# New orders for the first loads, stage A and the first full block of stage B in a two-attention kernel

## The chip, the cores and the metric

The kernel runs on one core of a Trainium2 chip. The metric is the device time of one execution in microseconds (us), as the median of several runs. The engines are TensorE (PE in the profile, with PEld for its weight loads), the vector engine (DVE), ScalarE (ACT), GpSimd (POOL) and SyncE (SP), which issues all transfers of this kernel.

## The reference

Two multi-head attentions on separate inputs, A and B, with 2048 tokens, width 512 and 32 heads of 16. A is causal with a sliding window of 256 tokens; B is full attention. The results stand side by side in the output.

```python
qkv = (x @ wqkv).reshape(B, S, 3, H, Dh).transpose(2, 0, 3, 1, 4)
q, k, v = qkv[0], qkv[1], qkv[2]
scores = einsum("bhqd,bhkd->bhqk", q, k) * Dh ** -0.5
# A only: key 0 to 255 tokens behind the query
scores = where((i - j >= 0) & (i - j < 256), scores, -1e9)
o = einsum("bhqk,bhkd->bhqd", softmax(scores), v)
y = o.transpose(0, 2, 1, 3).reshape(B, S, D) @ wo
out = concatenate([yA, yB], axis=-1)
```

All inputs are float32.

## The kernel before

**Tiling.** The tokens of each attention are cut into 4 chunks of 512 and 16 tiles of 128. Heads go in 8 groups of four. A *unit* is one attention, one group and one query chunk: 32 units of A, then 32 of B. Float32 accuracy comes from splitting each operand into a high part (a copy in a reduced format, on ScalarE) and a low part (the rest, a subtraction on DVE or GpSimd); a projection multiplies high by high, high by low and low by high over four blocks of 128 inputs, 12 matmuls in all (`products`, line 217 in the profile). The splits of A's first tiles are lines 170 (ScalarE) and 171 (DVE), and the loads that feed them line 185 (`load_split`).

**Steps.** A projection of queries or keys (`project_qk`) leaves its result in PSUM, ScalarE copies it out (line 275 for the first pair), the two parts are stored to DRAM, and loads bring them back laid out by head. Values (`project_v`) go through DRAM as well. For each unit, query times key matmuls are first done to find each row's maximum on DVE (line 454 for A, with lines 463 and 464; line 406 for B, with DVE's maximum in line 410), the negated maxima become extra rows of the query operand (a transpose, line 539 or 492), and then the scores are multiplied again with those rows (line 572), ScalarE takes the exponential (line 579), and the weighing with the values follows (line 603 for B, 618 for A). Output projections (`project_out`) run on TensorE between the scores of B; they use line 217 too.

**Stage A and its order.** `ORDER_A` is a string with one letter for each piece of TensorE's work: p a projection, m maxima of two heads, t the transposed rows of maxima, s the scores of two heads, w a weighing, e and S early work of B. `ORDER_P` names the projections in the order in which the p's take them: "Av20" is attention A, values, chunk 2, tile 0; "Ak01" is A, keys, pair 0, chunk 1. So TensorE's order is written out by hand. The order on ScalarE, DVE, GpSimd and SP is not: while the program is built, the class `Model` keeps an estimated time for each engine, and a step behind a load or a projection (a split, a copy out, a store, a load) is put into the program when the model's TensorE time has passed the step's own estimated time. Every engine then executes its instructions in that program order, waiting for whatever each needs. `Model.dma` estimates when a load lands: 0.45 us for its issue, 0.6 us more, 4 ns for each KB, and 1.3 us at the end.

**The first loads.** The list "load" is worked off in order: query weights of pair 0, the four 128-row tiles of token chunk 0 (as 1, 1 and 2), key weights of pair 0, constants, then two loads each of two tiles for chunk 1, two for the values' weights, and two for each of chunks 2 and 3. The tiles of two use staging buffers with the tag "p", of which there are six (`2 * AHEAD`), and a seventh load waits until the first of them has been split.

**Stage B and its order.** Here the order comes from short strings that are repeated. `ORDER` covers two key tiles (eight scores, two steps); "s" is the scores of one head, "M" the maxima of two heads in a fixed pair of banks (3 and 4), "m" the maximum of one head in a bank that it shares with the output projections, a digit a weighing of that many quarters, "T" the rows of maxima, and "x" one matmul of an output projection. `ORDER_F` covers eight steps with 12 x, and it is taken at each multiple of eight steps as long as an output projection is due. After 12 x one more matmul of the projection is issued. The first output projection is due from step 24 on. 16 blocks of `ORDER_F` follow one another from there, and then `ORDER` again. `ORDER_B`, `ORDER` without its last M, is for the block at two steps ahead of such a multiple, when a projection is due by then.

Of the kernel before, what the change touches and what calls it, by code (L numbers as in the profile page):

```python
# [20 lines left out]
HG = 4  # L21
# [17 lines left out]


ORDER = "ssm4mssMs2msms2TsM"
ORDER_B = "ssm4mssMs2msms2Ts"
ORDER_F = "msMs2mssm2ssMms4ssMms4ssMms4ssMsm4ssMms4mssMsxxxxxxTxxMsmss4MssmsxxxxsMsms4s"
LAST = "ssss4T"
LAST_F = "xxxxssss44ssssxxxxxxssss44ssssxx"
# [2 lines left out]


ORDER_P = (  # L50
# [4 lines left out]
    "Bk31 Bq30 Bq33 Bq32 Bq20 Bk23 Bk30 Bq31 Bk11 Bk33 Bk32 Bq12 ").split()  # L55
FIRST = 4.0
FINAL = 34.5
LOADS = 4.0
# [4 lines left out]


ORDER_A = (
    "pppppppmpmmpmmpmmmptpmmpmmpsmspmmpmsppmmpmmmpmmtpmsswmmmpsmswtmmpmswssmpmmtpmswmsmpmsswsmwssmpmswmss"
    "wtmmpsmmpsmwmmmpmsmwsmwsstpsmswmmmpsmswwssmpsmsptwsmmpmsmwwmsmpsmsptsmwmsmwsmsmsmwssmmwtssmwmmmpmswm"
    "msptsmmswmmmpmmswsmsmwsmtwsspssmwmmmpmsswtmswmsmpmsswmmswsmmptssmwmmspmsmwmswmsmpsmswmmmptmsmmmpmsmw"
    "smmswmswstmmpmsmsmwsmwsmssmwtmmmpmsmsmwssmwsmtswsmmpmswsmswmmtpsmswmmmpmsswmmmpmmtpsmswwmssptmswsmmw"
    "sspmswmmmpmsswsmtpmmswsmwsmmpmsssmwsmswmmtpssmwmmmpsmswmmmpsmswwsmmptsmwmsmpmsmwmsptsmwmsmpsmsptmswm"  # L70
    "mmpssmwmsmwsmsmwmsmptsmwmsmpsmswmmmpssmwmmmpssmtwwssmpmsswsmwsmmptsewmmmpsempsmswsemwsmptsewmmmpemsp"
    "mmswsmtwssepssmwmmmpempesswemmpssmwwsesptsmwemmpesmwmmpssmwsseptmsmpmmmpesmwsmwsmmpemmpmmmpemmpssmws"
    "mmptsmwmmmpSmSwmSmwSm")
LAND = 700
LATE = 1000
LAND_V = 2000
# [3 lines left out]


WAKES = {"PE": 226, "ACT": 243, "DVE": 219, "Pool": 200, "SP": 200, "DMA": 200}
TURN = {("f", "h"): 90, ("h", "f"): 85, ("h", "c"): 88, ("c", "h"): 115, ("c", "f"): 115, ("f", "c"): 105, ("c", "c"): 24}


class Model:
# [4 lines left out]
    def __init__(self):  # L91
        self.t = {e: 0 for e in ("PE", "ACT", "DVE", "Pool", "SP", "DMA")}
        self.mode, self.turn = "f", 170
        self.banks = {"e": [0] * 7, "o": [0]}
        self.lanes = [0] * 8

    def run(self, engine, ns, *after):
        self.t[engine] = max(self.t[engine], *after, 0) + ns
# [8 lines left out]
        self.mode = mode  # L107
        return self.run("PE", turn + ns, *after)

    def dma(self, kb, *after):  # L110
        t = self.run("SP", 450, *after, self.lanes[0]) + 600
        self.t["DMA"] = max(self.t["DMA"], t) + int(4.0 * kb)

        self.lanes = [*self.lanes[1:], self.t["DMA"] + 1300]
        return self.lanes[-1]
# [33 lines left out]
def attention_kernel(ctx: ExitStack, tc: tile.TileContext, xT, wqk, wv, wo, out):  # L149
# [9 lines left out]
    M = Model()  # L159
    ready = {}  # L160
    obank = [None]
    ns = 0
# [14 lines left out]
    def load_split(srcs, tags, d, keys, stage):  # L177

        slots = staged[stage]
        if stage == "p":  # L180
            r = sb.tile([128, 2, QC], F32, name=f"in_{keys[0]}".translate(NAMES), tag=stage, bufs=2 * AHEAD)
        else:
            r = sb.tile([128, QC], F32, name=f"in_{keys[0]}".translate(NAMES), tag=stage,
                        bufs=5 if stage == "row" else 3)[:, None]
        nc.sync.dma_start(r[:, :len(keys)], srcs)
        t = M.dma(256 * len(keys), slots.pop(0))

        def rest():
            for n, (tag, key) in enumerate(zip(tags, keys)):
                d[key] = sb.tile([128, 2, 512], F32R, name=f"{tag[0]}_{key}".translate(NAMES), tag=tag[0], bufs=tag[1])  # L190
                split(r[:, n], d[key], nc.gpsimd if stage == "stage" else nc.vector, key[:2] == (1, "o"))
                ready[tag[0], *key] = M.run(*(("Pool", 1260) if stage == "stage" else ("DVE", 602)),
                                            M.run("ACT", 500, t))
            slots.append(ready[tag[0], *key])
        after(t + (LAND_X if stage == "stage" else 0), rest, (stage, *keys[0]))
# [674 lines left out]
        list_("load", yes, free("p"), load_x, 0, 0, i, n)  # L870
    list_("load", yes, free("row"), load_wqk, 0, 0, 1)
    list_("load", yes, at0, constants)
    for n, f, *a in [(0, load_x, 0, 1, i, 2) for i in (0, 2)] + [(0, load_wv, 0, i, 2) for i in (0, 2)] + [
            (EARLY + 4 * (c - 2), load_x, 0, c, i, 2) for c in (2, 3) for i in (0, 2)]:
        list_("load", lambda n=n: nb >= n, free("p"), f, *a)
    list_("load", lambda: nb >= 12, at0, ones_out)
# [69 lines left out]
    nm = k = nb = ne = n1 = 0  # L946
# [18 lines left out]
    while todo_a or gen[0]:  # L965
# [8 lines left out]
        i, j = divmod(ns, HG)  # L974
        t = NEVER
        if gen[0]:
            t = pe
        elif x == "p":
            t = max(bank(), operands(bursts[nb][1]))
        elif x == "t" and nts:  # L980
            t = max(ready["nm", *nts[0]], bank())
        elif x == "w" and k < i:
            un, (m, pieces), a, z = flat[k]
            t = max(*(ready.get(("v", 0, un[1] // 2, y[0]), NEVER) for y in pieces), ready["p", *un, m],
                    M.bank("o") if a else 0)
        elif x == "s" and i < k + AHEAD and (max_rows, *flat[i][0]) in made:
            t = max(M.bank("e", 1), ready["q", *flat[i][0]] + LAND)
        elif x == "S" and ns == HG * len(flat) and len(flat) + n1 // HG < k + AHEAD and (max_rows, 1, 0, 0) in made:
            t = max(M.bank("e", 1), ready["q", 1, 0, 0] + LAND)
# [3 lines left out]
        elif x == "m" and not (mxs[nm][2] and (nts or mxs[nm][0][0] and ne < len(early))):  # L993
# [3 lines left out]
            t = max(t, M.pair()[0])  # L997
# [91 lines left out]
    ns, nq, nm, fed = n1, n1 - 8, AHEADM, 0  # L1089
    half, odd, full = 2 * AHEADM, None, set()  # L1090
    t0 = M.t["PE"] - 1000 * ns // HG * STEP
    rows, order = [], ORDER
    for u, g, c, qt, kc in mx[:AHEADM]:
        chunk_max(g, c, qt, kc)

    def due():
        return gen[0] or proj and proj[0][0] <= ns // HG * STEP and operands(proj[0][3]) <= M.t["PE"]

    while nq < 4 * len(steps):
        if nm == len(mx) and len(M.banks["e"]) == 3:  # L1100
            M.banks["e"] += [M.t["PE"] + 4000] * 2
        if nm == len(mx):
            order = LAST_F if due() and not rows else LAST
        else:
            f, g = order == ORDER_F, ns // HG % 8
            order = ORDER_F if due() and g == 0 and nm + 8 <= len(mx) else ORDER
            if order == ORDER and not f and g == 6 and due() and nm + 10 <= len(mx):
                order = ORDER_B
        for x in order:
            k = ns // HG  # L1110
            if x == "s" and k < len(steps):
                if ns % HG == 0:
                    t = k * STEP
                    M.t["PE"] = max(M.t["PE"], t0 + int(1000 * k * STEP))
                    settle()
                    while todo and todo[0][0] <= t:
                        pop()
                scores(1, *steps[k], ns % HG)
                ns += 1
            elif x in "Mm" and (half < 2 * len(mx) or x == "m" and odd is not None):  # L1120
                if x == "M":
                    y = half
                    half += 1
                    max2(*mx[y // 2][1:], (2 * (y % 2), 2 * (y % 2) + 1), ps_all[:, 3:5])
                elif odd is None:
                    y, odd = half, half
                    half += 1
                    max2(*mx[y // 2][1:], (2 * (y % 2),), room()[1][:, None])
                else:
                    y, odd = odd, None  # L1130
                    max2(*mx[y // 2][1:], (2 * (y % 2) + 1,), room()[1][:, None])
                if y != odd:
                    full.add(y)
                while {2 * nm, 2 * nm + 1} <= full:
                    u, g, c, qt, kc = mx[nm]
                    chunk_max(g, c, qt, kc)
                    nm += 1
                    if nm % 16 == 0:
                        low_finish(g, c)
                        rows.append((k + 1, (1, g, c)))  # L1140
            elif x == "T":
                if rows and rows[0][0] + (nm == len(mx)) <= k:
                    max_rows(*rows.pop(0)[1])
            elif x == "x" and (gen[0] or due()):
                now[0] = k * STEP
                advance()
                fed += 1
                if fed == 12:
                    fed = 0
                    advance()  # L1150
                    if nm < len(mx):
                        t0 += 2410
            elif x.isdigit():
                if 0 <= nq < 4 * len(steps):
                    g, c, kt = steps[nq // 4]
                    q = nq % 4
                    weigh2(g, c, kt, 128 * q, 128 * (q + int(x)))
                    if kt == NT - 1 and q + int(x) == 4:
                        unit_end(1, g, c)
                nq += int(x)  # L1160
# [29 lines left out]
```

## Time and profile before

| what | value |
|---|---|
| median of 3 runs | 1818.7 us (1818.28 to 1819.19) |
| the profiled execution, its own time | 1819.65 us |
| its span, first to last instruction | 1817.9 us |
| mean granted TensorE clock | 0.998 |
| first matmul | 10.19 us into the span |
| stage A | to about 535 us |
| stage B | from about 535 us on |
| maxima of B end | at about 1730 us |

Times in the profile count from the start of the span; the 1.75 us between the span and the execution's own time lie around it. A busy TensorE in the profile is not TensorE at its peak, since matmuls are pipelined and their ends are modelled. The granted clock is a share of the full clock.

### The profile page before, as it was taken

The numbers are of one execution on the slowest core, as the hardware profiler recorded it, in microseconds if no ns is written. First come the engines' busy times: TensorE is split into PE (matmuls) and PEld (weight loads), VectorE is DVE, ScalarE is ACT, GpSimd is POOL, SyncE is SP. The second block draws the span as 40 slices with busy tenths as digits, with TensorE's granted clock in tenths as the row PEclk, the third lists the DMA queues.
The fourth block names the chain that finished last, engine by engine and source line by source line (L and its number), as shares of the span: only waits on it lengthen the run. The fifth ranks groups of instructions, "written<-read, shape, count | busy, mean of one in ns | idle before, by whom it ended". The sixth has DMA issues, their size and how long they took to land. (4 is left out here: it accounts for less than half of the span.)

```text
span 1817.9 us, 38163 instructions
## 1 busy us (share of the span) xinstructions
PE 1798.2 (99%) x13992; PEld 901.4 (50%) x13992; DVE 1515.2 (83%) x2189; ACT 1420.0 (78%) x2773; POOL 688.8 (38%) x2054
## 2 busy tenths in 40 slices
PE   7999999999999999999999999999999999999999
PEld 5766666666664444444444444444444444444446
DVE  4655676766689889999989999999999999999911
ACT  4367777565659788888889988998898998899883
POOL 0167787554655453223222423332222333222310
PEclk9999999999999999999999999999999999999999
DMA  7756767454553225111300311030030121000012
GB/s 239 198 177 200 225 206 220 152 164 140 180 182 104 71 74 117 45 42 40 75 28 26 74 47 39 29 78 17 16 76 29 35 63 37 17 24 15 30 34 97
DMA packets 128569, 166.47 MB, mean 92 GB/s; under 512 B 22946, under 2 KB 58258, under 8 KB 128370
## 3 DMA queue, kind: packets, MB, share of 16 engines
q1 hardware_dynamic: 128382, 164.04, 31.2%
q8 instruction: 110, 1.80, 0.4%
q14 instruction: 77, 0.63, 0.1%
HBM read 94.49 MB, written 68.19 MB: 89 GB/s over the span
## 5 line engine op out<-in xcount | busy, mean ns | idle before, releaser
L579 ACT ACTIVATE p<-ps_all 128x512 f32<-128x512 f32 x2432 | 1257.8, 598 | 163.1 <-PE ps_all L572 116.0
L410 DVE TENSOR_REDUCE mt<-ps_all 128x1 f32<-128x512 f32 (+1 forms) x1482 | 1203.4, 884 | 53.3 <-PE ps_all L406 38.2
L572 PE MATMUL ps_all<-oq,opk 51*128 51x512 f32 (+3 forms) x2752 | 739.4, 406 | 2.4 <-ACT p L579 2.1
L406 PE MATMUL ps_all<-opk,oq 48*128 48x512 f32 x2016 | 636.3, 433 | 1.0 <-DVE mt L410 1.0
L603 PE MATMUL ps_all<-p,vt 128*32 128x256 f32 (+1 forms) x5672 | 586.8, 487 | 0.0
L572 PEld LDWEIGHTS ps_all<-oq,opk 51*128 51x128 f32 (+1 forms) x2752 | 376.8, 185 | 227.7 <-ACT p L579 196.0
L406 PEld LDWEIGHTS ps_all<-opk,oq 48*128 48x128 f32 x2016 | 303.1, 185 | 277.7 <-issue 149.7
L517 POOL TENSOR_TENSOR md<-mt,mm 128x4 f32<-128x4 f32 x372 | 75.9, 204 | 612.2 <-DVE mt L410 611.2
L589 POOL TENSOR_SCALAR_AFFINE_SELECT p<-p 128x256 f32<-128x256 f32 x480 | 178.9, 406 | 221.9 <-ACT p L579 220.4
L603 PEld LDWEIGHTS ps_all<-p,vt 128*32 128x32 f32 x5672 | 112.7, 108 | 218.1 <-issue 208.1
L217 PE MATMUL ps_all<-x,w 128*128 128x512 f32 x768 | 195.1, 404 | 10.3 <-ACT w L170 10.2
L463 DVE COPY_PREDICATED ps_all<-mone,ps_all 128x256 f32<-128x256 uint16 x224 | 95.0, 424 | 85.8 <-PE ps_all L454 84.1
L217 PEld LDWEIGHTS ps_all<-x,w 128*128 128x128 f32 x768 | 141.2, 190 | 50.5 <-ACT w L170 10.2
L464 DVE TENSOR_REDUCE mt<-ps_all 128x2 f32<-128x512 f32 x224 | 155.2, 693 | 7.7
L279 ACT ACTIVATE raw<-ps_all 128x512 f32<-128x512 f32 x56 | 33.5, 598 | 108.8 <-PE ps_all L217 105.9
L217 PE MATMUL ps_all<-w_o,x_o 128*128 128x512 f32 x384 | 102.3, 407 | 0.2 <-ACT ob L715 0.2
L217 PE MATMUL ps_all<-w_v,x 128*128 128x512 f32 x384 | 96.4, 400 | 0.3 <-DVE w_v L171 0.3
L618 PE MATMUL ps_all<-p,vt 128*32 128x384 f32 (+2 forms) x1408 | 96.4, 390 | 0.0
L518 POOL TENSOR_SCALAR md<-md 128x4 f32<-128x4 f32 x372 | 81.7, 220 | 32.6
L454 PE MATMUL ps_all<-opk,oq 48*128 48x384 f32 (+2 forms) x512 | 88.1, 373 | 1.3 <-DVE mt L464 1.1
L519 POOL TENSOR_TENSOR mm<-mm,md 128x4 f32<-128x4 f32 x372 | 74.8, 201 | 31.0
L217 PEld LDWEIGHTS ps_all<-w_o,x_o 128*128 128x128 f32 x384 | 68.0, 188 | 26.9 <-issue 8.0
(63 smaller groups left out, 718.3 us busy)
## 6 DMA issues: line engine op xcount, KB each, us to landing
parts<-st SPq DMA_DIRECT2D x64, 512.0 KB
opk<-parts SPq DMA_DIRECT2D x128, 128.0 KB
oq<-parts SPq DMA_DIRECT2D x128, 128.0 KB
od<-ou SPq DMA_DIRECT2D x64, 256.0 KB
vd<-vst SPq DMA_DIRECT2D x32, 272.0 KB
opk<-parts SPq DMA_DIRECT2D x128, 64.0 KB
oq<-parts SPq DMA_DIRECT2D x128, 64.0 KB
t<-od SPq DMA_DIRECT2D x32, 256.0 KB
```

What stands on the lines that cost most here:

```text
L217: nc.tensor.matmul(ps, l(u), r(v), start=start and k == 0, stop=stop and k == n - 1)
L406: nc.tensor.matmul(ps[:, n], q[rows, 128 * qt:128 * qt + 128], k[rows, kc * QC:kc * QC + QC], start=True, stop=True)
L410: nc.vector.tensor_reduce(out=m[:, a:a + len(heads), r, qt, kc], in_=ps, axis=AX.X, op=ALU.max)
L454: nc.tensor.matmul(two[:, a, 0:w], opq[b, g, c][rows, r, 128 * qt:128 * qt + 128], opk2(g)[rows, r, t0:t1], start=True, stop=True)
L463: nc.vector.copy_predicated(two[:, :, 256:384], later, two[:, :, 0:128])
L464: nc.vector.tensor_reduce(out=m[:, :, r, qt, 0], in_=two[:, :, 128:384], axis=AX.X, op=ALU.max)
L518: nc.gpsimd.tensor_scalar(d, d, 0.0, None, op0=ALU.max)
L572: nc.tensor.matmul(ps[x][:, col:col + n1], opk2(g)[rows, pr, 128 * k:128 * k + 128], opq[b, g, c][rows, pr, q0:q0 + n1], start=True, stop= ...
L579: nc.scalar.activation(p[:, a0 + x, :w], ps[x][:, :w], AF.Exp, scale=SCALE)
L589: nc.gpsimd.affine_select(out=v, in_=v, pattern=[[0, 2], [sign, 128]], compare_op=ALU.is_ge, fill=zero_fill, base=base, channel_multiplier ...
L603: nc.tensor.matmul(o[32 * j:32 * j + 32, q0:q1], vt[(g // 2) % 2][:, kt, vc:vc + 32], pts[1, g, c, kt, j // 2][:, j % 2, q0:q1], start=kt ...
L618: nc.tensor.matmul(o[32 * j:32 * j + 32, q0:q0 + w], vt[(g // 2) % 2][:, kt, vc:vc + 32], pts[b, g, c, m, j // 2][:, j % 2, col:col + w], ...
```

## The change

The values' weights are loaded ahead of token chunk 1 instead of behind it. `Model` gets a table of landing times for the first nine loads that go through `load_split`, in place of its formula. `ORDER_A` and `ORDER_P` are replaced. `ORDER_B` goes, and the first block that would be `ORDER_F` is `ORDER_F1` instead; the later ones stay.

```diff
--- before.py
+++ after.py
@@ -39,7 +39,7 @@
 
 
 ORDER = "ssm4mssMs2msms2TsM"
-ORDER_B = "ssm4mssMs2msms2Ts"
+ORDER_F1 = "ssm4msMss2msms2sMssm4ssmMs4mssm3mssMm14sssmMxxxxxxmssMsxTxxxxxsmMss2smms2sMssm4s"
 ORDER_F = "msMs2mssm2ssMms4ssMms4ssMms4ssMsm4ssMms4mssMsxxxxxxTxxMsmss4MssmsxxxxsMsms4s"
 LAST = "ssss4T"
 LAST_F = "xxxxssss44ssssxxxxxxssss44ssssxx"
@@ -48,11 +48,11 @@
 
 
 ORDER_P = (
-    "Ak00 Aq00 Av00 Av11 Aq01 Av20 Ak01 Aq02 Av02 Av33 Av13 Ak02 Av03 Av01 Ak03 Av31 Aq03 Av22 Av23 Av21 Av10 "
-    "Av12 Ak10 Av30 Ak11 Av32 Ak20 Ak13 Ak12 Aq10 Aq11 Aq12 Aq13 Aq20 Ak30 Ak21 Aq31 Aq30 Aq32 Aq21 Ak31 Ak23 "
-    "Bk00 Aq22 Ak32 Ak22 Aq33 Aq23 Ak33 Bq01 Bk01 Bq00 Bk02 Bk03 Bq02 Bv00 Bv33 Bv21 Bv31 Bv01 Bq13 Bk10 Bv32 "
-    "Bk13 Bq10 Bk12 Bq03 Bv02 Bv22 Bv13 Bv12 Bv30 Bq21 Bv23 Bk22 Bv20 Bv11 Bq11 Bv03 Bv10 Bk20 Bk21 Bq23 Bq22 "
-    "Bk31 Bq30 Bq33 Bq32 Bq20 Bk23 Bk30 Bq31 Bk11 Bk33 Bk32 Bq12 ").split()
+    "Aq00 Ak00 Av11 Av00 Ak01 Av01 Aq01 Ak02 Av03 Av21 Av33 Aq02 Av02 Aq03 Av12 Av10 Ak03 Av30 Av32 Av23 Av20 "
+    "Av13 Ak10 Ak11 Av22 Av31 Ak20 Aq12 Ak30 Ak12 Aq10 Ak13 Aq13 Aq11 Aq21 Aq30 Aq22 Aq20 Ak22 Aq31 Aq32 Ak21 "
+    "Ak31 Bk00 Ak32 Ak33 Ak23 Aq33 Aq23 Bk01 Bq01 Bq03 Bk02 Bk03 Bq00 Bv12 Bv22 Bv00 Bq02 Bv21 Bk21 Bv11 Bq13 "
+    "Bv31 Bv03 Bq12 Bk10 Bk20 Bv01 Bk13 Bq10 Bv10 Bv23 Bv20 Bv02 Bq23 Bk22 Bv13 Bv33 Bk23 Bq20 Bv32 Bv30 Bk11 "
+    "Bk12 Bq30 Bk30 Bk31 Bq31 Bq33 Bq11 Bk32 Bq21 Bk33 Bq32 Bq22 ").split()
 FIRST = 4.0
 FINAL = 34.5
 LOADS = 4.0
@@ -63,14 +63,14 @@
 
 
 ORDER_A = (
-    "pppppppmpmmpmmpmmmptpmmpmmpsmspmmpmsppmmpmmmpmmtpmsswmmmpsmswtmmpmswssmpmmtpmswmsmpmsswsmwssmpmswmss"
-    "wtmmpsmmpsmwmmmpmsmwsmwsstpsmswmmmpsmswwssmpsmsptwsmmpmsmwwmsmpsmsptsmwmsmwsmsmsmwssmmwtssmwmmmpmswm"
-    "msptsmmswmmmpmmswsmsmwsmtwsspssmwmmmpmsswtmswmsmpmsswmmswsmmptssmwmmspmsmwmswmsmpsmswmmmptmsmmmpmsmw"
-    "smmswmswstmmpmsmsmwsmwsmssmwtmmmpmsmsmwssmwsmtswsmmpmswsmswmmtpsmswmmmpmsswmmmpmmtpsmswwmssptmswsmmw"
-    "sspmswmmmpmsswsmtpmmswsmwsmmpmsssmwsmswmmtpssmwmmmpsmswmmmpsmswwsmmptsmwmsmpmsmwmsptsmwmsmpsmsptmswm"
-    "mmpssmwmsmwsmsmwmsmptsmwmsmpsmswmmmpssmwmmmpssmtwwssmpmsswsmwsmmptsewmmmpsempsmswsemwsmptsewmmmpemsp"
-    "mmswsmtwssepssmwmmmpempesswemmpssmwwsesptsmwemmpesmwmmpssmwsseptmsmpmmmpesmwsmwsmmpemmpmmmpemmpssmws"
-    "mmptsmwmmmpSmSwmSmwSm")
+    "pppppppmmppmmpmmmpmpmmptpmmpmmpssspmmpmmpsmtpmsswmmmpsmmpmmmptmswmsmpwmmsptmswmsmpsmswsmwmmmpmsspmms"
+    "wsmwmsmptmswssmpmsmwsmwssmptmswmmmpmsswmstwmsspwmmmpmsspmmswwmsmpsmsptsmmwsmmswsmswtsmmswmsswmmpsmsw"
+    "mmpmsstwmmmpmswsmmswsstwmspsmswmmmpsmmswmsmwmsptsmswmmmpmsmwtmsswsmmpsmsmwmmmptsmsmwmmmpssmwmmmptsmm"
+    "swssmwmsmwsmpmssmwsmstwmssmwmmmpmssmwmsmwtssmwmsmpmsmwsmptsmwmsmpssmwmmmpsmswsmmptmswmswsmmptmswmsmp"
+    "msswsmwmsmpmmswsmwmsmptssmwmsmpsmswsmswmmtpsmswmmmpsmswssmwwsmmptmswsmmpmswsmmpmmswsmptsmwmsmpmswmsm"
+    "pmswmmmpsssptmmptsmwsmswsmswmmmpssmwmmmpsmswwmsmptmswmmmpsmwmsmpseswmmspsseptsmwmmmpemmpsmswtmswmmmp"
+    "tsmwmmmpssepseswseswmmmpesswemmptsesmwwmmmpesspmmswsmwmmmpssmwmmmptseswemmpemmpemmpseswsempsmswmmmpm"
+    "mmptsmswsmmpSmSwSmwSm")
 LAND = 700
 LATE = 1000
 LAND_V = 2000
@@ -80,6 +80,7 @@
 
 
 WAKES = {"PE": 226, "ACT": 243, "DVE": 219, "Pool": 200, "SP": 200, "DMA": 200}
+LANDINGS = 3500, 5400, 6100, 8300, 9300, 10400, 11800, 13200, 14600
 TURN = {("f", "h"): 90, ("h", "f"): 85, ("h", "c"): 88, ("c", "h"): 115, ("c", "f"): 115, ("f", "c"): 105, ("c", "c"): 24}
 
 
@@ -93,6 +94,7 @@
         self.mode, self.turn = "f", 170
         self.banks = {"e": [0] * 7, "o": [0]}
         self.lanes = [0] * 8
+        self.landings = list(LANDINGS)
 
     def run(self, engine, ns, *after):
         self.t[engine] = max(self.t[engine], *after, 0) + ns
@@ -107,9 +109,11 @@
         self.mode = mode
         return self.run("PE", turn + ns, *after)
 
-    def dma(self, kb, *after):
+    def dma(self, kb, *after, first=False):
         t = self.run("SP", 450, *after, self.lanes[0]) + 600
         self.t["DMA"] = max(self.t["DMA"], t) + int(4.0 * kb)
+        if first and self.landings:
+            self.t["DMA"] = self.landings.pop(0) - 1300
 
         self.lanes = [*self.lanes[1:], self.t["DMA"] + 1300]
         return self.lanes[-1]
@@ -183,7 +187,7 @@
             r = sb.tile([128, QC], F32, name=f"in_{keys[0]}".translate(NAMES), tag=stage,
                         bufs=5 if stage == "row" else 3)[:, None]
         nc.sync.dma_start(r[:, :len(keys)], srcs)
-        t = M.dma(256 * len(keys), slots.pop(0))
+        t = M.dma(256 * len(keys), slots.pop(0), first=True)
 
         def rest():
             for n, (tag, key) in enumerate(zip(tags, keys)):
@@ -870,7 +874,7 @@
         list_("load", yes, free("p"), load_x, 0, 0, i, n)
     list_("load", yes, free("row"), load_wqk, 0, 0, 1)
     list_("load", yes, at0, constants)
-    for n, f, *a in [(0, load_x, 0, 1, i, 2) for i in (0, 2)] + [(0, load_wv, 0, i, 2) for i in (0, 2)] + [
+    for n, f, *a in [(0, load_wv, 0, i, 2) for i in (0, 2)] + [(0, load_x, 0, 1, i, 2) for i in (0, 2)] + [
             (EARLY + 4 * (c - 2), load_x, 0, c, i, 2) for c in (2, 3) for i in (0, 2)]:
         list_("load", lambda n=n: nb >= n, free("p"), f, *a)
     list_("load", lambda: nb >= 12, at0, ones_out)
@@ -1089,7 +1093,7 @@
     ns, nq, nm, fed = n1, n1 - 8, AHEADM, 0
     half, odd, full = 2 * AHEADM, None, set()
     t0 = M.t["PE"] - 1000 * ns // HG * STEP
-    rows, order = [], ORDER
+    rows, first = [], True
     for u, g, c, qt, kc in mx[:AHEADM]:
         chunk_max(g, c, qt, kc)
 
@@ -1102,10 +1106,10 @@
         if nm == len(mx):
             order = LAST_F if due() and not rows else LAST
         else:
-            f, g = order == ORDER_F, ns // HG % 8
+            g = ns // HG % 8
             order = ORDER_F if due() and g == 0 and nm + 8 <= len(mx) else ORDER
-            if order == ORDER and not f and g == 6 and due() and nm + 10 <= len(mx):
-                order = ORDER_B
+            if order is ORDER_F and first:
+                order, first = ORDER_F1, False
         for x in order:
             k = ns // HG
             if x == "s" and k < len(steps):
```

## The prediction

> **What bounds the kernel now.** I read the page first (span and busy engines), then the waits of TensorE, then busy time and granted clock by stretch, then the order of time at the two places where TensorE stands still longest.
>
> ```profile
> span 1817.9 us, 38163 instructions
> PE 1798.2 (99%) x13992; PEld 901.4 (50%) x13992; DVE 1515.2 (83%) x2189; ACT 1420.0 (78%) x2773; POOL 688.8 (38%) x2054
> ...
> PE ps_all L217 <- ACT w L170: 10.2, 1, 10.2
> PE ps_all L572 <- ACT p L579: 2.1, 8, 0.5
> PE ps_all L454 <- DVE mt L464: 1.1, 3, 0.5
> PE ps_all L406 <- DVE mt L410: 1.0, 1, 1.0
> ```
>
> TensorE is busy in 99% of the span, and only 19.7 us (1817.9 less 1798.2) are left. So a new order gains only what it takes out of TensorE's waits or out of its slow stretches. Two waits stand out: 10.2 us before the first matmul, put down to the split of a weight tile, and one of 1.0 us on the maxima of the vector engine (DVE). All other waits are 0.5 us at most.
>
> ```profile
> 45.00:535.00 490.00, 487.62 (x3720) 324.17 (x3718) 329.14 (x680) 299.98 (x591) 292.17 (x571) 1.00 0.61 185
> ...
> 182.00:273.00 91.00, 89.17 (x718) 57.46 (x717) 66.37 (x156) 65.30 (x131) 71.14 (x126) 1.00 0.72 215
> 364.00:455.00 91.00, 90.99 (x728) 60.54 (x730) 60.51 (x135) 53.70 (x104) 45.71 (x104) 1.00 0.49 152
> ...
> 592.00:595.90 3.90, 2.90 (x24) 1.34 (x20) 3.90 (x5) 2.24 (x4) 3.58 (x6) 1.00 0.61 146
> 595.90:602.73 6.83, 6.83 (x36) 2.25 (x36) 3.96 (x6) 3.88 (x8) 4.60 (x11) 0.50 0.10 35
> ```
>
> These are stretches: length, then busy time of PE, PEld, DVE, ACT and POOL, then clock. The first row is stage A, in which TensorE idles 2.4 us in 490; the worst 91 us of it idle 1.83 us, a good stretch 0.01. The last two rows are the only slow stretch: right behind the 1.0 us wait, the granted clock is 0.50 for 6.83 us, so half of that, 3.4 us, is lost there.
>
> **The change, part by part.**
>
> *The start.* The first projection was Ak00 and becomes Aq00. The row of waits names the weight tile of Ak00, which is loaded fifth; the weights of Aq00 are loaded first.
>
> ```profile
> 3.67 0.63 ACT L170 ACTIVATE w<-in 128x512 fp32r<-128x512 f32 x1 [1.61 <-DMA in<-wqk_A]
> 5.58 1.29 ACT L170 ACTIVATE x<-in 128x512 fp32r<-128x512 f32 x2 [1.28 <-DMA in<-xT_A]
> 8.47 1.15 ACT L170 ACTIVATE x<-in 128x512 fp32r<-128x512 f32 x2 [1.60 <-DMA in<-xT_A]
> 9.53 0.61 ACT L170 ACTIVATE w<-in 128x512 fp32r<-128x512 f32 x1
> 10.49 1.15 ACT L170 ACTIVATE x<-in 128x512 fp32r<-128x512 f32 x2 [0.35 <-DMA in<-xT_A]
> 11.85 1.15 ACT L170 ACTIVATE x<-in 128x512 fp32r<-128x512 f32 x2 [0.22 <-DMA in<-xT_A]
> 15.76 0.60 ACT L275 ACTIVATE st<-ps_all 128x512 fp32r<-128x512 f32 x1 [2.75 <-PE ps_all L217]
> 16.25 1.14 ACT L170 ACTIVATE w_v<-in_v 128x512 fp32r<-128x512 f32 x2
> ...
> 6.24 1.36 DVE L171 TENSOR_TENSOR x<-in,x 128x512 fp32r<-128x512 f32 x2 [1.22 <-ACT x L170]
> 9.13 1.29 DVE L171 TENSOR_TENSOR x<-in,x 128x512 fp32r<-128x512 f32 x2 [1.54 <-ACT x L170]
> 10.34 0.68 DVE L171 TENSOR_TENSOR w<-in,w 128x512 fp32r<-128x512 f32 x1
> ...
> 10.19 8.32 PE L217 MATMUL ps_all<-x,w 128*128 128x512 f32 x24 [10.19 <-ACT w L170]
> 18.35 1.87 PE L217 MATMUL ps_all<-w_v,x 128*128 128x512 f32 x7
> 24.49 2.88 PE L217 MATMUL ps_all<-x,w 128*128 128x512 f32 x12
> ...
> 10.19:15.52 5.33, 5.33 (x13) 4.01 (x14) 1.00 1.05 392
> 15.52:18.35 2.83, 2.83 (x14) 2.31 (x12) 1.00 0.29 111
> ```
>
> The first three parts are ScalarE, DVE and TensorE in order of time; the last two rows are line 217 by stretch. One projection is 12 matmuls. The first takes 5.33 us (0.444 us each), the second 2.83 (0.236 each): TensorE starts at about half pace, although the clock column has no drop. The same four projections stand first in both orders (Ak00, Aq00, Av00, Av11), and before they end at 24.49.
>
> Aq00 can start when the first token tile's high part is there, 6.24 instead of 10.19. At slow pace it ends at 6.24 + 5.33 = 11.6; the fourth tile's low part is there at 9.13 + 1.29 = 10.4, in time. Ak00's weights are there at 10.34 + 0.68 = 11.0, so it ends at 14.4 at the full pace and at 17.0 at the slow one. Next is Av11, which needs the second token chunk. Here the moved load counts: its 2 transfers go past the 2 of the chunk on SP's queue, and 4 splits on ScalarE and 4 on DVE change places with the chunk's 4 and 4. The chunk's halves were split on landing at 10.49 and 11.85, 1.36 apart; two transfers later they come at 13.2 and 14.6. The seventh load still waits for a free staging buffer, now the chunk's second half in place of the weights' second half: the same wait in the same place. ScalarE's splits of the last half take 1.15 us, DVE's end 0.7 later, so about 16.4, or 17.0 if ScalarE first takes Ak00's result (0.6). So Av11 ends about 17.5 (last tile at 17.0 plus two matmuls), Av00 2.8 later at 20.3: a gain of 4.2. With Ak00 at the slow pace to 17.0, ScalarE stands behind it as it did at 15.76 (2.75 us idle), the chunk is split by 19.6, Av11 ends at 20.1 and Av00 at 22.9: a gain of 1.6. I take **3.2**, a little nearer to the first, since the slow pace ended 5.3 us behind the first matmul, but the new first matmuls lie farther apart. What the weights gain by their earlier split (16.25 before) is in this sum. All later work follows these projections, and TensorE is full behind them, so I let the gain go through to the end.
>
> [...]
>
> *The landing table.* It changes no instruction, only where ScalarE, DVE and SP take their work in the program: nothing by itself, beyond the start and stage A as costed.
>
> *The order of stage A.* The counts are equal (96 projections, 284 maxima, 192 scores, 96 weighings, 33 rows), and changes of matmul kind go from 366 to 365. Projections are only permuted. If all of stage A idled as its good stretch does, it would gain 2.4 us; if all of it idled as its worst (1.83 in 91), it would idle 9.9 us, a loss of 7.5. With the same counts I take **0**. What hides the moved work is PSUM's seven banks; without them each maximum waits for DVE as below.
>
> *The first full block of stage B.* ORDER_F1 takes the place of ORDER_F once; ORDER_B goes. ORDER_B was for a block at step 22 with an output projection due, but the first is due at step 24, and the trace has the closing M which ORDER_B leaves out: zero.
>
> ```profile
> 591.46 0.64 PE L603 MATMUL ps_all<-p,vt 128*32 128x256 f32 x8
> 592.03 0.94 PE L406 MATMUL ps_all<-opk,oq 48*128 48x512 f32 x3
> 592.81 0.40 PE L572 MATMUL ps_all<-oq,opk 51*128 51x512 f32 x1
> 594.21 0.50 PE L406 MATMUL ps_all<-opk,oq 48*128 48x512 f32 x2 [1.00 <-DVE mt L410]
> ...
> 592.81:618.66 25.85, 10.73 (x32) 4.84 (x32) 0.87 0.12 36
> 618.66:639.65 20.99, 9.40 (x33) 4.41 (x32) 1.00 0.32 102
> 639.65:661.62 21.97, 9.43 (x33) 4.43 (x32) 1.00 0.33 79
> 1100.00:1118.80 18.80, 10.68 (x32) 5.32 (x32) 1.00 0.05 18
> ...
> L410 DVE TENSOR_REDUCE mt<-ps_all 128x1 f32<-128x512 f32 x40 | 25.5, 677 | 0.0
> L410 DVE TENSOR_REDUCE mt<-ps_all 128x2 f32<-128x1024 f32 x20 | 24.3, 1216 | 0.0
> ```
>
> The first part is TensorE in order of time. The second is line 572 by stretch, 32 scores or eight steps each: the first ORDER_F block takes 25.85 us, the next two 20.99 and 21.97, eight steps of plain ORDER 18.80. The last two rows are DVE's maxima in 46 us of ORDER, which they fill (49.8 us; starts overlap the ends before).
>
> ORDER closes with an M and ORDER_F opens with "msM". Both M use the same two banks, so the second waits until DVE has done the first, the m between them behind it: 593.21 to 594.21. ORDER_F1 opens as ORDER does ("ssm4ms", then M). Its M lie 3, 5, 4, 5 and 3 scores apart, from the closing M of ORDER up to the first x. ORDER keeps up with M about every 4 scores, 2.3 us. Up to its 17th score ORDER_F1 has 4 M and 9 m; its DVE work, 4 × 1.14 + 9 × 0.60 = 10.0 us (durations less the overlap of 0.07), fits the 17/4 × 2.35 = 10.0 us that ORDER takes for as many. The one close pair has "m14" between, five quarters of weighing (two quarters take 0.57 us, from 591.46 to 592.03), 1.4 us. So I expect no wait over half a microsecond there.
>
> Its length: it has the 8 M and 16 m of four ORDER blocks, so 18.80, plus 13 output matmuls at 0.236, 3.1 us: 21.9. That is also in the upper half of what ORDER_F needs when undisturbed, and ORDER_F1 has 11 weighings against 9. Gain 25.85 − 21.9, **4.0**. Bounds: 4.9 if it runs in 20.99; nothing if a new wait halves the clock again.
>
> **Sum.** 3.2 + 0 + 4.0 = 7.2 us. The profiled execution took 1819.65 us, 1.75 more than its span, so 1812.4 by its own time; it lies 0.95 above the median of the runs, and against the median, 1818.7, the forecast is **1811.5 us**. 0.2% is 3.6 us, about what a measurement of this kernel can tell from no change.
>
> **Rivals.**
>
> *The slow clock comes anyway.* The drop could belong to the passage (two kinds of few-row matmuls and then output matmuls) and not to the wait. Then only the 1.0 us wait goes, less 0.4 for more weighings: 3.2 + 0.6, 1814.9. For it: the drop began 1.7 us behind the end of the wait. Against it: the same kinds of matmul run at 1.00 in all later blocks. [...]
>
> *The chunk comes late.* ScalarE waits behind Ak00's result, Av11 takes the time that Aq00 won, and the start gains nothing: 1818.7 − 4.0 = 1814.7. For it: ScalarE stood 2.75 us in just that way. Against: it would need Av11 to end at 21.7, 1.6 us beyond my slow case.
>
> *Slower: runs of three maxima.* The new order has 28 runs of three m against 25. If a third m waits a microsecond for DVE and the clock halves, each such place costs 1.0 + 3.4 = 4.4 us. From the third place on it decides: 13.2 − 7.2 = 6.0 slower, 1824.7. For it: line 454 already waits for DVE, up to 0.5 us. Against: 25 such runs cost 1.1 us and no clock.
>
> *It does not do what it says.* DVE or transfers make up both gains by longer waits in stage A (its worst stretch everywhere, 7.5): 1818.9, say 1818.7.
>
> **How the numbers follow.** Chances: forecast 0.64, slow clock anyway 0.12, late chunk 0.10, slower 0.07, nothing 0.07. The two middle cases gain 3.8 and 4.0 us, at the edge of 3.6, so half of each counts as the same. Faster 0.64 + 0.11 = 0.75; same 0.07 + 0.11 = 0.18; slower 0.07. Low end: 4.2 + 4.9 + 2.4 = 11.5 gives 1807.2; TensorE's waits under half a microsecond lie in no row, so I go to 1806.5. High end: both middle cases and about 2 us of worse stage A, 1817.0. Outside are the last two cases and some tails, 0.2. The forecast's own range is 1807 to 1814.
>
> **What would show it.** Right: first matmul near 6.2; the fifth projection near 21; no 1.0 us wait of line 406; no stretch at 0.50 behind the first matmuls; ORDER_F1's 32 scores in about 22 us. Wrong: the fifth projection later than 23, line 406 or 454 waiting a microsecond, a second stretch at half clock, or stage A idling over 5 us behind its start.

## The result and the profile after

| | before | after |
|---|---|---|
| median of five executions | 1818.77 us (four of them 1818.28 to 1819.19) | 1809.57 us (1808.29 to 1811.50) |
| ratio, with its 95% interval | 1 | 0.9947 (0.9936 to 0.9957) |
| profiled execution, its own time | 1819.65 us | 1809.57 us |
| its span | 1817.9 us | 1807.8 us |

One execution of the kernel before took 3173.76 us, and the ratio is taken over the fast executions alone. Ratios here and below are the ones on record; they can differ by up to 0.0004 from the quotient of the medians shown, which is 0.9950 here.

The change makes the kernel 9.2 us faster in the median, 10.1 us between the two profiled executions. The same views of the changed kernel follow; its lines stand 4 further down, so 217, 406, 454, 539 and 572 of before are 221, 410, 458, 543 and 576. First the page and TensorE's waits:

```profile
span 1807.8 us, 38196 instructions
PE 1793.0 (99%) x14008; PEld 901.4 (50%) x14008; DVE 1515.5 (84%) x2191; ACT 1419.8 (79%) x2773; POOL 688.6 (38%) x2054
```

```profile
PE ps_all L221 <- ACT x L174: 5.8, 2, 5.4
PE ps_all L543 <- POOL nm L533: 1.7, 2, 1.2
PE ps_all L458 <- ACT p L583: 1.1, 3, 0.5
```

The first wait is 5.4 us in place of 10.2. The 1.0 us wait on DVE's maxima is gone, and a new one of 1.2 us has come, for the transposed rows of maxima (line 543). The start in order of time, ScalarE and then TensorE:

```profile
4.68 0.63 ACT L174 ACTIVATE x<-in 128x512 fp32r<-128x512 f32 x1 [0.49 <-DMA in<-xT_A]
```

```profile
10.28 1.15 ACT L174 ACTIVATE w_v<-in_v 128x512 fp32r<-128x512 f32 x2 [0.29 <-DMA in_v<-wv_A]
12.27 0.60 ACT L279 ACTIVATE st<-ps_all 128x512 fp32r<-128x512 f32 x1 [0.83 <-PE ps_all L221]
12.76 1.14 ACT L174 ACTIVATE w_v<-in_v 128x512 fp32r<-128x512 f32 x2
13.80 1.14 ACT L174 ACTIVATE x<-in 128x512 fp32r<-128x512 f32 x2
15.43 0.60 ACT L279 ACTIVATE st<-ps_all 128x512 fp32r<-128x512 f32 x1 [0.49 <-PE ps_all L221]
```

```profile
5.36 3.22 PE L221 MATMUL ps_all<-x,w 128*128 128x512 f32 x6 [5.36 <-ACT x L174]
9.00 6.39 PE L221 MATMUL ps_all<-x,w 128*128 128x512 f32 x18 [0.42 <-ACT x L174]
15.23 6.08 PE L221 MATMUL ps_all<-w_v,x 128*128 128x512 f32 x24
21.14 2.88 PE L221 MATMUL ps_all<-x,w 128*128 128x512 f32 x12
```

The first four projections end at 21.14 in place of 24.49. The rest by stretch (length, then busy time of PE, PEld, DVE, ACT, POOL, then clock): of before, from the fifth projection to the first score of B, from there to step 24, and the first full block; then the same three of after.

```profile
24.49:535.02 510.53, 507.67 (x3810) 339.17 (x3808) 338.55 (x707) 306.25 (x602) 292.17 (x571) 1.00 0.62 187
535.02:592.81 57.79, 57.45 (x491) 24.31 (x491) 55.66 (x72) 52.35 (x103) 30.96 (x87) 1.00 0.46 125
592.81:618.66 25.85, 24.85 (x150) 9.79 (x150) 20.39 (x24) 17.46 (x34) 12.63 (x32) 0.87 0.12 36
```

```profile
21.14:528.41 507.27, 505.20 (x3813) 339.55 (x3811) 340.56 (x708) 307.32 (x604) 292.89 (x572) 1.00 0.63 189
528.41:586.19 57.78, 56.26 (x489) 23.72 (x488) 53.95 (x70) 51.09 (x100) 29.60 (x85) 1.00 0.46 124
586.18:608.31 22.13, 22.13 (x169) 9.91 (x167) 20.49 (x27) 17.46 (x35) 12.60 (x33) 1.00 0.21 60
```

So the 10.1 us are 3.35 at the start (24.49 − 21.14), 3.26 in the rest of stage A, nothing up to step 24, 3.72 in the first full block; the remaining stretches, 318.2 and 881 us long in both, give back 0.25.

### The profile page after: what moved, and what is told of

Read it like the earlier page. It is cut to its first block, busy times and chain, and to the rows that moved or that the text cites. A ratio compares the mean times of both kernels' runs of the same rounds, so it can differ in the third digit from the quotient of the medians.

```text
span 1807.8 us, 38196 instructions
## 1 busy us (share of the span) xinstructions
PE 1793.0 (99%) x14008; PEld 901.4 (50%) x14008; DVE 1515.5 (84%) x2191; ACT 1419.8 (79%) x2773; POOL 688.6 (38%) x2054
```

## The experiments

Eight kernels take apart the first full block, the start, the table, the loads, the orders and a wait that came new with the change; four more followed from what these showed. Kernels on different chips are compared by their ratios to the kernel before.

**ORDER_F1 alone.** `before` with the new string and its two lines in the loop.

```diff
+ORDER_F1 = "ssm4msMss2msms2sMssm4ssmMs4mssm3mssMm14sssmMxxxxxxmssMsxTxxxxxsmMss2smms2sMssm4s"
...
-    rows, order = [], ORDER
+    rows, order, first = [], ORDER, True
...
+            if order is ORDER_F and first:
+                order, first = ORDER_F1, False
```

> The kernel before with ORDER_F1 alone. Own theory (the double M makes TensorE wait, and the wait halves the clock): the first full block takes about 22.1 us in place of 25.9, no 1.0 us wait of line 406 or its like, no stretch at half clock, 1815.0 us in all. Rival (the slow clock belongs to the passage): the block still has some 6.8 us at 0.50, only the wait goes, 1818.2 us.

1815.99 us against 1819.76, ratio 0.9979 (0.9970 to 0.9988). Line 573 of this kernel by stretch, the 32 scores of the first full block:

```profile
592.23:614.40 22.17, 10.27 (x33) 4.66 (x33) 1.00 0.22 60
```

The kernel gains 3.8 us, and the block takes 22.17 us in place of 25.85 at full clock: the term of the new string, by itself. All eleven executions had a mean clock of 1.000. The rival that the slow clock comes anyway has fallen.

**The double M taken away in another way.**

```diff
-            if order == ORDER and not f and g == 6 and due() and nm + 10 <= len(mx):
+            if ns // HG == 22:
                 order = ORDER_B
```

> The kernel before with its own ORDER_F, but the block ahead of the first one leaves out its closing M (ORDER_B put there by step number), so that the two M no longer stand side by side; that M is made up later, nothing is left out. Own theory: the wait goes and the clock with it, the first full block takes 21 to 22.2 us, 1814.6 us (1814.0 to 1815.5). Rival (slow clock belongs to the passage, ORDER_F or what follows): clock still at 0.50 behind step 24, about 1817.8. Second rival (ORDER_F1's even spacing is what helps): the wait of a microsecond comes at the next M, about 1818.5.

1837.60 us, ratio 1.0097 (1.0083 to 1.0110): 18 us slower, which no theory had. The block itself does as my theory said. Line 572 over its 32 scores, and the longest of TensorE's waits over the whole kernel:

```profile
592.44:614.16 21.72, 9.18 (x33) 4.16 (x31) 1.00 0.13 44
```

```profile
PE ps_all L539 <- POOL nm L529: 18.4, 29, 1.0
```

ORDER_F without a double M takes 21.72 us at full clock, so the pair was the cause there, and ORDER_F1's spacing isn't needed for it. But the M left out stays one block behind to the end, and the last maximum of nearly every unit then comes too late for the "T" behind it: 29 waits of line 539, 18.4 us. ORDER_F1 keeps the M.

**The double M put back.**

```diff
-            if order is ORDER_F and first:
-                order, first = ORDER_F1, False
```

> The changed kernel with ORDER_F also for the first full block. Own theory: wait of about 1.0 us and half clock come back behind step 24, block of 25.9 us, 1809.6 + 3.7 = 1813.3 us. Rival (the new stage A leaves the block in another state, or the clock's phase decides): block of 22 to 23 us, 1810.2 us.

1811.75 us, ratio 0.9959 (0.9945 to 0.9972), 1.7 us over the changed kernel on the same chip (1810.07, ratio 0.9948, below), not 3.7; the two intervals overlap, so even the 1.7 us are not certain. TensorE in order of time; line 576 over the 32 scores of the block; all engines in the 3.4 us behind the wait:

```profile
587.23 0.50 PE L410 MATMUL ps_all<-opk,oq 48*128 48x512 f32 x2 [1.00 <-DVE mt L414]
```

```profile
585.84:608.71 22.87, 9.60 (x32) 4.36 (x32) 1.00 0.13 41
```

```profile
589.40:592.80 3.40, 3.40 (x32) 1.46 (x28) 3.13 (x5) 2.95 (x7) 3.17 (x5) 1.00 0.10 36
```

The wait is back to the hundredth, but the clock stays at 1.00, and the block takes 22.87 us: 0.7 more than ORDER_F1's 22.13, and 1.15 more than ORDER_F's 21.72 without the pair, which is about what the wait costs. Of the five executions one had a mean clock of 0.997 (1814.37 us), the others 1.000. So the slow clock that mostly follows the wait in the kernel before (58 of its 61 executions on these two chips had a mean clock under 1.000, and the three at 1.000 took 1816.0 to 1817.4) is not certain. My theory is right on the wait and half right on the clock.

**Aq00 first, alone.**

```diff
-    "Ak00 Aq00 Av00 Av11 Aq01 ...
+    "Aq00 Ak00 Av00 Av11 Aq01 ...
```

> The kernel before with Aq00 and Ak00 exchanged, nothing else: the first projection takes the weights that land first. Own theory (the first wait is all of the start's gain): first matmul at 5.4 to 6.2 us, the fifth projection at 21.5 to 23 (before 24.49, after 21.14), as Av00 now waits for the values' weights that are still loaded behind the second chunk; 1818.8 - 2.2 = 1816.6 us. Rival (the start needs the loads' order and the table as well): fifth projection at 24 or later, 1818.5 us.

1819.45 us, ratio 0.9999 (0.9990 to 1.0008): nothing. My theory fell. The profile is of the slowest of the eleven executions (1823.57 us). ScalarE, then TensorE, then TensorE by stretch up to the fifth projection:

```profile
10.20 0.62 ACT L170 ACTIVATE w<-in 128x512 fp32r<-128x512 f32 x1
13.09 0.60 ACT L275 ACTIVATE st<-ps_all 128x512 fp32r<-128x512 f32 x1 [2.28 <-PE ps_all L217]
```

```profile
5.56 3.23 PE L217 MATMUL ps_all<-x,w 128*128 128x512 f32 x6 [5.56 <-ACT x L170]
17.04 0.50 PE L217 MATMUL ps_all<-w_v,x 128*128 128x512 f32 x1 [1.21 <-ACT w_v L170]
18.60 7.14 PE L217 MATMUL ps_all<-w_v,x 128*128 128x512 f32 x23 [1.06 <-DVE w_v L171]
25.57 2.88 PE L217 MATMUL ps_all<-x,w 128*128 128x512 f32 x12
```

```profile
15.83:19.81 3.98, 1.72 (x7) 1.00 0.68 258
19.81:23.22 3.41, 3.41 (x9) 0.50 0.12 45
23.22:25.57 2.35, 2.35 (x11) 1.00 0.40 119
```

The first matmul starts 4.6 us earlier, and the fifth projection 1.1 us later than before. ScalarE has split the last weight by 10.8 and then stands 2.28 us before Aq00's copy out, with the next tiles' splits queued behind it; so they come late, and the third projection waits for them twice. Behind these waits the clock is at 0.50 for 3.41 us, which costs 1.7; without that the fifth projection would have begun at about 23.9 (an estimate), 0.6 us earlier than before. So the exchange alone wins at most a small part of the 4.6 us, and in this execution it loses.

**The table taken out of the changed kernel.**

```diff
-        self.landings = list(LANDINGS)
+        self.landings = []
```

> The changed kernel with an empty landing table, so that the model goes by its formula and ScalarE, DVE and SP take the first splits and stores in another order. Own theory: a difference of at most 1 us at the start, 1809.6 to 1810.6 us. Rival (the table is what makes the early work fit): fifth projection 1 to 3 us later and longer waits to 90 us, 1812 us or more.

1814.79 us, ratio 0.9977 (0.9968 to 0.9986): 5 us of the gain gone; the rival was right. ScalarE, then TensorE:

```profile
12.74 0.60 ACT L279 ACTIVATE st<-ps_all 128x512 fp32r<-128x512 f32 x1 [2.28 <-PE ps_all L221]
13.24 2.18 ACT L174 ACTIVATE w_v<-in_v 128x512 fp32r<-128x512 f32 x4
16.54 0.60 ACT L279 ACTIVATE st<-ps_all 128x512 fp32r<-128x512 f32 x1 [1.13 <-PE ps_all L221]
```

```profile
17.71 6.12 PE L221 MATMUL ps_all<-w_v,x 128*128 128x512 f32 x24 [1.20 <-ACT x L174]
23.67 2.88 PE L221 MATMUL ps_all<-x,w 128*128 128x512 f32 x12
```

The same picture: the copy out of Aq00 stands ahead of all four splits of the values' weights, where the changed kernel has two of them ahead of it (10.28 and 12.27 above). The third projection starts at 17.71 in place of 15.23 and the fifth at 23.67; then a 0.57 us wait at 42.7 is followed by 3.41 us of half clock.

**The old load order in the changed kernel.**

```diff
-    for n, f, *a in [(0, load_wv, 0, i, 2) for i in (0, 2)] + [(0, load_x, 0, 1, i, 2) for i in (0, 2)] + [
+    for n, f, *a in [(0, load_x, 0, 1, i, 2) for i in (0, 2)] + [(0, load_wv, 0, i, 2) for i in (0, 2)] + [
```

> The changed kernel with the values' weights loaded behind the second chunk again. Own theory (Av11 comes third and needs both the second chunk and the values' weights, whichever lands last, so the exchange of the loads is worth nothing): fifth projection at 21.1 within 0.3, 1809.6 us within 1. Rival (the load move is a part of the start's gain): fifth projection 1 to 3 us later, 1811 to 1813 us.

1811.14 us, ratio 0.9955 (0.9942 to 0.9967) against 0.9947; profiled span 1807.1 us, fifth projection at 20.61. No loss shows, which fits that Av11 needs the values' weights and the second chunk, whichever lands last. The moved load brought nothing that can be measured.

**The old orders in the changed kernel.** Both strings, ORDER_A and ORDER_P, as before.

> The changed kernel with ORDER_A and ORDER_P of before: new load order, table and ORDER_F1 alone. Own theory (the new orders bring the start's 3.35 and stage A's 3.3 us): first matmul still near 10.2, Av00 third with its weights there earlier (up to 0.7 us gained), stage A from the fifth projection on as long as before (510.5 us), 1814.4 us. Rival (the table and the loads' order shorten stage A): 1811.5 us.

1819.50 us, ratio 1.0004 (0.9996 to 1.0013), slower than both theories said: ORDER_F1's gain is there (first block 22.17 us), and it is spent in stage A. The start gains 1.2 us (fifth projection at 23.32), but then

```profile
PE ps_all L458 <- DMA oq<-parts: 2.2, 1, 2.2
```

at 31.6 us, and 3.41 us at half clock behind it (mean clock of this execution 0.999). Stage A from the fifth projection on takes 514.4 us; without these two, 2.2 + 1.7, it would be 510.5 as before.

**Table and exchange, two by two.** The table's lines put into the kernel before, with and without the exchange of Ak00 and Aq00; load order and the rest as before.

> The kernel before with Aq00 and Ak00 exchanged and the landing table, with the old load order and all else as it was. Own theory after the exchange alone failed (what counts is where ScalarE's copies out of a projection stand among its splits, and the table moves them): the fifth projection begins at 21.1 us (before 24.49, the exchange alone 25.57), Av00 no longer waits a microsecond for a split. Rival (the new third projection Av11 or the new load order is needed): 23.5 us or later. The rest of stage A keeps an order that was made without the table and may lose 0 to 4 us, so 1816 to 1820 us in all.

> The kernel before with the landing table alone. Own theory (the table is worth something only where projections end among the splits): first matmul still near 10.2, Av00 without its 0.7 us of waits, fifth projection at 23.4 us, 1.1 before the old one. Rival (the table by itself brings most of the start): 22 us or earlier. Rest of stage A as above, 1818 to 1822 us in all.

With both, 1816.18 us, ratio 0.9980 (0.9971 to 0.9989); with the table alone 1824.19 us, ratio 1.0025 (1.0015 to 1.0035), slower than my range: its profile has a 3.43 us wait for `oq` at 31.9 us and 3.4 us at half clock behind it, 5.1 us together. ScalarE and TensorE with both:

```profile
10.13 1.15 ACT L174 ACTIVATE x<-in 128x512 fp32r<-128x512 f32 x2 [0.33 <-DMA in<-xT_A]
12.08 0.60 ACT L279 ACTIVATE st<-ps_all 128x512 fp32r<-128x512 f32 x1 [0.80 <-PE ps_all L221]
```

```profile
21.38 2.88 PE L221 MATMUL ps_all<-x,w 128*128 128x512 f32 x12
```

The fifth projection starts at

| | Ak00 first | Aq00 first |
|---|---|---|
| formula | 24.49 | 25.57 |
| table | 23.56 | 21.38 |

Each entry is one profile, and the 25.57 has 1.7 us of half clock in it, as shown above. The exchange saves 2.2 us with the table; by the formula it costs 1.1, or saves 0.6 without the half clock. Together the two give 3.1 of the start's 3.35 us, without the new load order or any other new order. So the start's gain needs both: TensorE's early begin pays when ScalarE's program has some of the next tiles' splits ahead of the first copy out. The table moves DVE's and SP's work too, which no run separates from ScalarE's.

**A 1.2 us wait of the changed kernel taken away.**

```diff
-                plan(... if b else 14 + 8 * (4 * c + p),
+                plan(... if b else 12 + 8 * (4 * c + p),
```

(the planned time of A's normalisations, in `normalise`'s plan).

> The changed kernel with A's normalisations planned 2 us earlier (12 in place of 14), so that GpSimd does the one at 557 us a maximum earlier and the rows of maxima at 561 us need not wait for it. Own theory (that 1.2 us wait of line 543 costs about 0.7 us of steps 2 to 24 and halves the clock in some executions, hence clocks of 0.999 in two of five): wait gone, clock 1.000 in every execution, 1807.8 us in the median. Rival (DVE is behind there anyway, and the clock drops elsewhere): 1809.6 us, and the clock is still 0.999 in some executions.

> The changed kernel itself, as a measure for the next one on the same chip: 0.9947 of the kernel before, executions up to 3 us apart, those with a granted clock of 0.999 or less being the longer ones.

> The changed kernel with A's normalisations planned 2 us earlier, beside the changed kernel on the same chip. Own theory (the 1.2 us wait for the rows of maxima at 561 us goes): 0.7 to 1.3 us below the changed kernel in the median. Rival (later blocks give it back): within 0.4 us of it.

First run: 1808.97 us, ratio 0.9941 (0.9928 to 0.9953). Side by side: the changed kernel 1810.07, 0.9948 (0.9935 to 0.9960), and this one 1809.61, 0.9943 (0.9930 to 0.9955). From B's first score to step 24, and the wait of line 543:

```profile
528.60:585.12 56.52, 56.22 (x489) 23.77 (x488) 53.92 (x70) 50.93 (x100) 31.25 (x85) 1.00 0.47 128
```

```profile
PE ps_all L543 <- POOL nm L533: 1.0, 2, 0.5
```

The first row, 57.78 us in the changed kernel, has become 56.52: the wait is gone, and 0.5 us comes back later, at 685.6 us, as another wait of line 543. The 1807.8 us that I had expected and, side by side, the 0.7 to 1.3 us did not come. All ten executions had a mean clock of 1.000, where the changed kernel had 0.999 in three of ten, too few to tell the two apart. It is the fastest of all kernels run, but by about 0.5 us, inside the intervals: a lead over the changed kernel isn't shown, one over the kernel before is.

## Why the prediction was right, and where it was not

The forecast was 1811.5 us, in a range of 1806.5 to 1817.0, and "faster" had most of the chance; 1809.57 came. The sum was 7.2 us against 9.2, or 10.1 by the profiled executions. Two of its three terms held in size; the third, stage A's order, was put at nothing and brought as much as either, so the total came out 1.9 us below the forecast.

*The start*, 3.2 forecast, 3.35 measured. That the two agree so closely is luck: three profiles with the start of before have the fifth projection at 23.98, 24.41 and 24.49 us, five with the start of the changed kernel at 20.54 to 22.20, which gives 2.9 us in the mean. The path was the one told: Aq00 ahead of Ak00, the chunk in time for Av11, ScalarE behind a copy out as the danger. The slow pace lasted 7.6 us behind the first matmul (first record of full clock at 13.00), between the 5.3 and 10.8 of my two cases. First matmul 5.36, not 6.2, since the first two tiles were split one by one as they landed. But the reason was incomplete. I put the landing table at nothing by itself, and the runs show that the exchange without it brings nothing (ratio 0.9999): the mechanism of the rival "the chunk comes late", ScalarE's splits behind the copy out, is what the exchange alone and the kernel without the table show. The moved load, which I costed at length, brought nothing measurable.

*Stage A's order*, 0 forecast, 3.26 measured: the term that was mis-sized, and the gain is beyond the 2.4 us that I took for the most. That bound came from the premise that a new order gains only what it takes out of TensorE's waits or slow stretches, and this step was wrong. Visible idle time went only from 2.9 to 2.1 us (the stretches above), so 2.5 us came out of intervals that count as busy. By the starts of the matmuls in the traces, from the fifth projection to the first score of B, the intervals that begin with one of A's maxima (line 454, 512 matmuls) sum to 70.5 us before and 68.2 after, those that begin with a score (line 572, 704 matmuls) to 64.7 and 63.6. That the maxima found free banks sooner would fit, but no run separates it, so the cause within the stage stays open. What the runs do show: six profiles with new orders and table have 507.1 to 507.3 us here, four with the old orders and no slow stretch in stage A 510.4 to 511.0, and the new orders without the table 510.9, of which 2.3 are the wait and the half clock at 42.7 us. So the gain goes with the new orders, 1.9 of the 3.3 us of it without the table.

*The first full block*, 4.0 forecast, 3.72 measured; 22.13 us against 21.9. The cause of the wait, two M on the same pair of banks, was shown in both directions: it goes with the pair and comes back with it. The clock's part, 3.4 us, was right for the kernel before, where it goes with the pair, but it is not certain behind the wait, as the double M put back showed.

*ORDER_B*, zero: the profile before has the M that it would leave out, and forcing it cost 18 us.

*Missed:* the 1.21 us wait of line 543 at 561 us, from GpSimd's normalisation, which the new timing put one maximum later. It cost up to 1.3 us in its stretch (57.78 against 56.52); the whole stretch still came out even with the kernel before.

## What to carry to other kernels

When a program's order on one engine is written by hand and the others' by an estimate, an earlier start on the first may bring nothing unless the estimate moves the others' queues too: here the same exchange of two projections brought 2.2 us with the new estimates and nothing in the median with the old. Two pieces that share a buffer should not meet where one repeated pattern ends and the next begins; look at the seam, and keep the total of each kind of work, since one deferred maximum cost 18 us over the rest of the kernel. Visible idle time is no upper bound on what a reordering can gain: 2.5 of the 3.3 us that the new order of stage A saved came out of intervals in which TensorE counted as busy. And look at the clock of a profile before comparing two starts: one drop of it made a small gain look like a loss.

## What the runs showed of the hardware

Six profiles have a mean granted clock under 1.000 (0.996 to 0.999). In the views of them the drops are stretches at about half clock: 6.83 us at 0.50 in the kernel before (from 595.90 us on), 3.41 at 0.50 with the exchange alone (from 19.81 on, above), 3.40 at 0.50 with the table alone (from 35.9 on). TensorE by stretch around two more, in the changed kernel without its table and in the kernel before with exchange and table:

```profile
42.00:45.50 3.50, 2.65 (x9) 1.00 0.87 241
45.50:48.91 3.41, 3.41 (x10) 0.50 0.94 243
```

```profile
590.30:593.73 3.43, 2.44 (x22) 0.99 0.52 123
593.73:597.14 3.41, 3.41 (x22) 0.51 0.28 77
```

The first drop came behind a wait of 0.57 us (projections and maxima around it), while 1.2 us before line 543 brought no drop in three profiles (the changed kernel, it with the double M and it with the old load order, mean clock 1.000 in each), nor did any of the 29 waits of line 539, up to 1.0 us, in the kernel without the double M (1.000). The 1.0 us wait of lines 406 and 410 was followed by 6.83 us of half clock in the kernel before, by 3.41 with exchange and table, and by none with the table alone (1.00 from 602.0 to 605.4 us) and with the double M put back (1.00 from 589.40 to 592.80, above). So the length of the wait alone does not decide it in these profiles; what else does stays open.

At the start, the first record of full clock lies at 15.64 us in the trace of the kernel before, 5.4 us behind its first matmul, and at 13.00 in that of the changed kernel, 7.6 us behind; there line 221 has 9 matmuls in the 3.58 us ahead of it and 12 in the 2.39 us behind. What sets this length was not shown, nor whether it makes the spread of the fifth projections above, 20.54 to 22.20 us.
